# Unpacking the channel weights in the second batch's first two slots and placing its channel groups between theta's products

## The chip, the cores and the metric

The kernel runs on one core of one Trainium2 chip. The metric is the device time of one execution in microseconds (us). A measurement of this kernel repeats to about 0.2%. Engines: PE is TensorE (matrix products), DVE is VectorE, ACT is ScalarE, POOL is GpSimd, SP is SyncE, whose queue starts nearly all transfers here.

## The reference, cut to what matters

For 8 batches of 8 heads, 576 positions and 64 values each: attention with a window of 128 positions and a slope per head; its output x (576 x 512 per batch) goes through a mixing block.

```python
theta = x @ w_theta                              # per batch 576 x 512 @ 512 x 512
zr, zi = x * np.cos(theta), x * np.sin(theta)
y = w_tok_r @ zr + w_tok_i @ zi                  # mixing over the 576 positions
u = x + y
out = u + np.maximum(u @ w_ch, 0.0)              # channels: 512 x 512
```

`w_theta`, `w_tok_r`, `w_tok_i` and `w_ch` arrive as 8-byte floats, which the chip's engines here turn into 4-byte words by integer operations ("unpacking"). Most products are made of three products of shorter words: a matrix is split into a high and a low part, and high x high, high x low and low x high are added.

## The kernel before, in words

Batches follow each other as a pipeline. While batch b+1 does its attention (`attend`), batch b's mixing products (`mix`) stand between that attention's products. Then `turn` of batch b+1 makes x's transposes, theta and the angles, and gives z as a high and a low part. Then batch b's channel products (`channels`) follow.

- `attend` (L814 on) has four slots, one for each pair of heads. A slot runs some steps of mixing, the scores of the next pair (`scores`, then `weigh`: DVE adds the bias and finds the least value, ACT takes the exponential), steps of mixing, `values` of the present pair, `finish` (L583 on: three DVE operations that leave x_sb), and steps of mixing. `flip` (L532 on) turns the next pair's weights: ACT makes the high half (L555), DVE the low half (L558), SP sends both through a transposing transfer to `pt`. `split_low` (L438, L440) makes the low parts of q and k for the pair after the next.
- One step of mixing is three products of 128 x 288 (L77); nine steps are one group, 72 steps a batch. After a group DVE folds the result in (L762), ACT makes u's high part (L764), POOL a scaled copy (L766) and u's low part (L767). How many steps stand where is written out by hand: `FIRST` (L33) for batch 0's mixing, four numbers for each slot. For batch 0 it places 66 steps; the other six stand in the turn of batch 1.
- `turn`'s `run` calls `between` six times: before the first transposes (`columns`), behind the transposes of the next tile of rows for four of the five tiles, and at the end. For batches after the first one, a channel group (12 products of 128 x 288: four with the weights' high part, four with the low part, four with u's low part) is placed at each call, and two more in the attention's last slots. For batch 0 the calls do other work (below), and its eight channel groups run in a row behind the turn of batch 1.
- The channel weights come in four parts of 512 KB (`LATE`). A step of `unpack` takes one part: `apart` (ACT L187, POOL L188), `together` (DVE L194, L197, L202, then ACT L203 sums the rows), and the load of the next part (SP L177). Part 0 is loaded ahead; parts 0 and 1 are unpacked in slot 0, part 2 in slot 1, part 3 in slot 2.
- From the row sums one number follows, the scale s of the channel weights: `sums_first` (DVE L347, L348), `spread_from` (a PE transpose of the peaks, DVE L313, L315), `sums_last` (a PE product with ones, DVE L158, L160, L354, L165). `split_channels` (L358 on) then splits the weights with it: ACT L362 writes wch_hi, DVE L363 wch_lo, each in two halves of 128 x 1024. All this stands in the turn of batch 1, at its calls 2 to 5.

PE runs strictly in the order of the program (`keep_in_program_order`). For the other engines a planner sets the order when the program is built: among what it thinks is ready, the earlier in the program goes first; `issue_after` and `behind_all` let an operation be issued only behind others; `high_priority` brings one forward. Each engine then works through its list in that order. PSUM has two pools: `ps_s` (2 buffers: scores, values, transposes of x) and `ps_m` (4 buffers: mixing, theta, channels, spreads).

Of the kernel before, what the change touches and what calls it, by code (L numbers as in the profile page):

```python
# [17 lines left out]
AF = mybir.ActivationFunctionType  # L18
# [11 lines left out]

DEPTH = 1

FIRST = ((3, 11, 6, 3), (4, 4, 5, 4), (4, 4, 5, 4), (4, 3, 2, 0))  # L33
STEPS, FINISH = ((7, 7, 4, 3), (3, 5, 7, 4), (3, 4, 6, 3)), 250

GROUP = 4
# [17 lines left out]
def attn_moe_kernel(ctx: ExitStack, tc: tile.TileContext, qk_in, vx, wth, wtok, wch_in, band, out):  # L54
    nc = tc.nc
# [35 lines left out]
    def behind_all(some):  # L91
        stack = ExitStack()
        for ins in some:
            stack.enter_context(tc.issue_after(ins.ins))
        return stack
# [249 lines left out]
    def sums_first():  # L345

        nc.vector.tensor_reduce(out=peaks[2][:, :1], in_=csums, axis=mybir.AxisListType.X, op=ALU.max)  # L347
        nc.vector.tensor_scalar(out=peaks[2][:, :1], in0=peaks[2][:, :1], scalar1=2.0 ** (WEXP - 1),  # L348
                                scalar2=2.0 ** -100, op0=ALU.mult, op1=ALU.max)

    def sums_last(diag):

        s = spread_to(diag, 1, "c")
        nc.vector.tensor_scalar(out=ratio[:, 1:2], in0=ratio[:, :1], scalar1=s, scalar2=None, op0=ALU.mult)  # L354
        inverse(ratio[:, 2:3], ratio[:, 1:2])
        return s

    def split_channels(s):  # L358

        for k in range(0, 4, 2):  # L360
            part = slice(k, k + 2)
            nc.scalar.activation(wch_hi[:, part], wch[:, part], AF.Copy, scale=s)  # L362
            nc.vector.scalar_tensor_tensor(out=wch_lo[:, part], in0=wch[:, part], scalar=s, in1=wch_hi[:, part],  # L363
                                           op0=ALU.mult, op1=ALU.subtract)

    def coming(b):
        return [g for g in (2 * b + 3, 2 * b + 4) if g < B * H // GROUP]
# [442 lines left out]
    def step(stream, k=1):  # L810
        for _ in range(k):
            next(stream, None)

    def attend(b, x_sb, mixing, chans, first, behind, lowered):  # L814

        for g in range(H // 2):
            p = b * H // 2 + g
            pair = first.pop(0)
            new = None
            if p + DEPTH < pairs:  # L820
                new = Pair(p + DEPTH)
                first.append(new)
            def scores(tiles):
                if new is not None:
                    with tc.issue_after(lowered.ins) if b == 1 and g == 0 else nullcontext():
                        new.scores(tiles, behind)

            steps = STEPS[min(g, 2)] if b > 1 else FIRST[g]
            step(mixing, steps[0])
            if g == 1:  # L830
                spread_scales(b - 1, diag)
            ahead = p + DEPTH + 1
            made = split_high(ahead, raw.pop(ahead)) if ahead < pairs else None
            for tiles in SCORES:
                scores(tiles)
            if made is not None:
                with tc.issue_after(new.weighed.ins):
                    parts[ahead] = split_low(made)
                    prepare(ahead + 1)
            if new is not None and not new.early:  # L840
                new.flip(0)
                if g:
                    new.flip(1)
            step(mixing, steps[1])
            if g == 0:
                diag = spread_first(b - 1)
            step(mixing, steps[2])
            pair.values()
            with tc.high_priority(FINISH):
                done = pair.finish(x_sb)  # L850
            if new is not None and (new.early or g == 0):
                new.flip(0 if new.early else 1, done)
            step(mixing, steps[3])
            if new is not None and new.early:
                new.flip(1)
            with tc.issue_after(done.ins):
                if new is not None:
                    new.heads[0].ready()
                if b == 1 and g == 0:
                    with behind_all(new.exps):  # L860
                        step(late)
            if g >= 2 and b > 1:
                step(chans)
            if new is not None:
                with tc.issue_after(done.ins):
                    done = new.heads[1].ready() or done
                    for low in lows:
                        after(low(), done)
                    if b == 1 and g < 3:
                        with behind_all(new.exps + [new.copied]):  # L870
                            step(late)
            else:
                for low in lows:
                    low()
            lows.clear()
            if new is not None and not new.early:
                sent[:] = [new.sent]
            if g == (1 if b == 1 else 0) or g == 2:
                g_v = 2 * b + 3 + g // 2
                if g_v < B * H // GROUP:  # L880
                    with behind_all(sent):
                        load_values(g_v)
# [88 lines left out]
    for b in range(B):  # L971
        chans = channels(b, st[b])
        mixing = mix(st[b])
        if b + 1 < B:
            x_sb = xp.tile([128, NT, DM], F32, name="x_sb")
            attend(b + 1, x_sb, mixing, chans, first, st[b]["turned"], st[b]["lowered"])
            if b:
                for _ in mixing:
                    pass
            if first:  # L980
                latest = first[-1].exps
            st[b + 1]["exps"] = latest
            calls, diags = [], []

            def between():
                calls.append(None)
                n = len(calls)
                if b:
                    step(chans)
                elif n == 1:  # L990
                    step(mixing, 3)
                elif n == 2:
                    for _ in mixing:
                        pass
                    for low in lows:
                        low()
                    lows.clear()
                    sums_first()
                elif n == 3:
                    diags.append(spread_from(peaks[2], 1, "c"))  # L1000
                elif n == 4:
                    diags.append(sums_last(diags[0]))
                elif n == 5:
                    split_channels(diags[1])

            turn(x_sb, st[b + 1])(between)
            for _ in chans:
                pass
        else:
            step(mixing, 45)  # L1010
            for _ in range(3):
                step(chans)
                step(mixing, 9)
            for _ in mixing:
                pass
            for _ in chans:
                pass
# [52 lines left out]
```

## Time and profile before

| what | value |
|---|---|
| time before, median of 3 runs | 631.06 us (630.17 to 631.55) |
| the profiled execution's own time | 630.1 us |
| its span, from first to last instruction | 628.3 us |
| PE busy | 600.3 us (96%) |
| DVE busy | 527.6 us (84%) |
| ACT busy | 486.3 us (77%) |
| POOL busy | 198.7 us (32%) |
| attention of batch 1 (four slots) | about 91 to 142 us in the span |
| turn of batch 1 | about 140 to 162 us |
| channels of batch 0 | 162.2 to 173.9 us |

Times in the rows are counted from the first instruction. A row of a timeline gives the start, the duration, the engine, the line, the operation and its tiles; what stands in brackets at its end is the idle time of the engine before it, and what ended it. Matmuls overlap, so what a matmul costs is the distance between starts. "Granted clock" is the share of full speed that TensorE was given.

### The profile page before, as it was taken

How to read it: one execution, taken by the hardware profiler on the slowest of the kernel's cores; microseconds unless marked ns; L12 is line 12 of the kernel's file. 1: busy time of each engine (PE TensorE's matmuls, PEld its weight loads, DVE VectorE, ACT ScalarE, POOL GpSimd, SP SyncE). 2: the span in 40 equal slices, each digit the busy share in tenths (PEclk: the TensorE clock that was granted, in tenths of full speed). 3: DMA queues.
4: the chain of work that ended last, by engine and by line, in shares of the span. 5: the costliest groups of instructions: out<-in, count | busy, mean ns of one | idle time of the engine just before them, and what ended most of it. 6: DMA issues, size and time to landing. Idle time of an engine off the chain costs nothing.

```text
span 628.3 us, 14876 instructions
## 1 busy us (share of the span) xinstructions
PE 600.3 (96%) x5727; PEld 493.3 (79%) x5727; DVE 527.6 (84%) x1350; ACT 486.3 (77%) x917; POOL 198.7 (32%) x252
## 2 busy tenths in 40 slices
PE   5799799988899999999999999999999999999997
PEld 3688578867688878888788878888788878887776
DVE  4788888999999988998899889997899879956733
ACT  3889878788688779896989689886998799727710
POOL 4433303442314402432224411541225322530200
PEclk9789989999999999999999999999999999999999
DMA  8952102794148930897059910995069802751001
GB/s 317 355 188 85 53 25 75 164 230 81 39 116 196 225 73 20 199 193 171 21 100 220 215 50 26 228 207 118 30 148 183 179 29 75 113 87 39 20 20 57
DMA packets 137847, 78.10 MB, mean 124 GB/s; under 512 B 110768, under 2 KB 127280, under 8 KB 137776
## 3 DMA queue, kind: packets, MB, share of 16 engines
q1 hardware_dynamic: 137776, 77.15, 51.0%
q8 instruction: 45, 0.74, 0.5%
q14 instruction: 26, 0.21, 0.1%
HBM read 40.44 MB, written 9.44 MB: 79 GB/s over the span
## 4 chain that ended last, share of the span: by engine, by line
PE 55%; DVE 18%; ACT 14%; DMA 3%; issue 2%; DVEq 0%; ACTq 0%
PE mm L77 44%; PE ps L77 9%; DMA pt<-hl 3%; DVE hl L558 2%; PE ps L102 2%; ACT back L530 2%; ACT hl L555 2%; ACT front L530 1%; ACT g L675 1%; DVE front L527 1%; DVE f L671 1%; ACT g L674 1%; DVE g L685 1%; DVE f L685 1%; DVE z_lo L624 1%
## 5 line engine op out<-in xcount | busy, mean ns | idle before, releaser
L77 PE MATMUL mm<-wtk_hi,z_hi 128*128 128x288 f16 x576 | 165.1, 287 | 0.0
L77 PE MATMUL mm<-wtk_lo,z_hi 128*128 128x288 f16 x576 | 164.7, 286 | 0.0
L77 PE MATMUL mm<-wtk_hi,z_lo 128*128 128x288 f16 x576 | 164.7, 286 | 0.0
L77 PEld LDWEIGHTS <-z_hi 128*128 128x128 f16 x1152 | 108.7, 98 | 29.4 <-issue 0.6
L766 POOL TENSOR_SCALAR us<-xtf,fixed 128x288 f32<-128x288 f32 x56 | 80.4, 1438 | 107.5 <-DVE xtf L762 105.1
L77 PE MATMUL mm<-u,wch_hi 128*128 128x288 f16 x512 | 81.1, 287 | 0.0
L530 ACT ACTIVATE front<-front,fixed 128x256 f32<-128x256 f32 (+2 forms) x160 | 60.5, 444 | 20.4 <-DVE fixed L527 20.1
L77 PEld LDWEIGHTS <-z_lo 128*128 128x128 f16 x576 | 56.4, 98 | 14.2
L77 PEld LDWEIGHTS <-wch_hi 128*128 128x128 f16 x512 | 48.1, 98 | 18.0 <-issue 6.9
L764 ACT ACTIVATE u<-xtf,fixed 128x288 f16<-128x288 f32 x64 | 33.5, 525 | 32.7 <-DVE xtf L762 32.7
L530 ACT ACTIVATE back<-back,fixed 128x256 f32<-128x256 f32 x128 | 56.4, 495 | 2.1 <-DVE fixed L527 2.1
L767 POOL TENSOR_TENSOR u<-us,u 128x288 f16<-128x288 f32 x56 | 43.0, 782 | 44.9 <-DVE vl L461 21.5
L77 PE MATMUL mm<-wth_hi,x_hi 128*128 128x512 f32 x160 | 47.5, 419 | 3.9 <-ACT x_hi L646 2.5
L624 POOL TENSOR_TENSOR z_lo<-g,z_hi 128x512 f16<-128x512 f32 x14 | 16.5, 1179 | 109.3 <-ACT z_hi L622 109.3
L77 PE MATMUL ps<-vh,pt 128*128 128x65 f16 x936 | 47.8, 194 | 2.8 <-DMA pt<-hl 1.6
L77 PEld LDWEIGHTS <-pt 128*128 128x128 f16 x1404 | 46.4, 98 | 4.9 <-DMA pt<-hl 2.3
L77 PE MATMUL ps<-kh,qh 64*128 64x256 f32 (+1 forms) x304 | 47.3, 351 | 1.8 <-DVE x_sb L596 0.9
L77 PE MATMUL ps<-vl,pt 128*128 128x64 f16 x468 | 45.9, 193 | 0.0
L762 DVE SCALAR_TENSOR_TENSOR xtf<-mm,fixed,xtf 128x288 f32<-128x288 f32 x64 | 32.0, 510 | 15.1 <-PE mm L77 15.1
L77 PE MATMUL mm<-wth_lo,x_hi 128*128 128x512 f32 x160 | 44.5, 399 | 0.0
L795 DVE SCALAR_TENSOR_TENSOR xtf<-mm,fixed,xtf 128x288 f32<-128x288 f32 x64 | 32.7, 512 | 13.1 <-PE mm L77 12.6
L77 PE MATMUL mm<-u,wch_lo 128*128 128x288 f16 x256 | 41.8, 286 | 0.0
(186 smaller groups left out, 1442.2 us busy)
## 6 DMA issues: line engine op xcount, KB each, us to landing
vb<-in_vx_dram SPq DMA_DIRECT2D x16, 650.0 KB, 5.2
out_dram<-xtf SPq DMA_DIRECT2D x64, 144.0 KB, 1.8
qr<-in_qk_dram SPq DMA_DIRECT2D x26, 320.0 KB, 3.0
kr<-in_qk_dram SPq DMA_DIRECT2D x26, 288.0 KB, 3.8
xtf<-in_wch_dram SPq DMA_DIRECT2D x4, 512.0 KB, 3.8
qh<-in_qk_dram SPq DMA_DIRECT2D x6, 320.0 KB, 5.8
kh<-in_qk_dram SPq DMA_DIRECT2D x6, 288.0 KB, 6.1
xtf<-in_wtok_dram SPq DMA_DIRECT2D x3, 576.0 KB, 9.2
```

The source lines that it names most:

```text
L77: ins = nc.tensor.matmul(*args, **kw)
L102: ins = nc.tensor.transpose(*args)
L530: self.exps.append(nc.scalar.activation(sb, sb, AF.Exp, bias=least, scale=-1.0))
L555: self.copied = nc.scalar.activation(hl[:, 0], src, AF.Copy, scale=2.0 ** PEXP)
L558: self.lowered = nc.vector.scalar_tensor_tensor(out=hl[:, 1], in0=src, scalar=2.0 ** PEXP, in1=hl[:, 0], op0=ALU.mult, op1=ALU.subtract)
L624: low = engine.tensor_tensor(out=z_lo[:, c, :], in0=z, in1=z_hi[:, c, :], op=ALU.subtract)
L685: nc.vector.scalar_tensor_tensor(out=z, in0=x_sb[:, i, :], scalar=zs[:, c:c + 1], in1=z, op0=ALU.mult, op1=ALU.mult)
L762: nc.vector.scalar_tensor_tensor(out=xtf[:, m, cs], in0=y_ps[:, :HALF], scalar=st["back"], in1=xtf[:, m, cs], op0=ALU.mult, op1=ALU.add)
L764: nc.scalar.activation(u_hi[:, m, cs], xtf[:, m, cs], AF.Copy, scale=up)
L766: nc.gpsimd.tensor_scalar(out=us[:, m, cs], in0=xtf[:, m, cs], scalar1=up, scalar2=None, op0=ALU.mult)
L767: lows.append(lambda m=m, cs=cs: nc.gpsimd.tensor_tensor(out=u_lo[:, m, cs], in0=us[:, m, cs], in1=u_hi[:, m, cs], op=ALU.subtract))
L795: nc.vector.scalar_tensor_tensor(out=xtf[:, e, cs], in0=o_ps[:, :HALF], scalar=down, in1=xtf[:, e, cs], op0=ALU.mult, op1=ALU.max)
```

## The change

Part 2 is unpacked in slot 1 at the first head and part 3 in slot 1 at the second (before: slot 1, second head, and slot 2, second head). `sums_first` follows in slot 1. `spread_from` stands behind slot 2's `finish`, `sums_last` behind the first mixing steps of slot 3, and the two halves of `split_channels` stand at slot 3's first and second head. All 72 mixing steps of batch 0 are now in the attention: slot 3 has (4, 4, 4, 3) in place of (4, 3, 2, 0). The calls of `between` in batch 1's turn place 0, 1, 1, 2, 2 and 1 channel groups of batch 0, and the eighth follows the turn.

```diff
-FIRST = ((3, 11, 6, 3), (4, 4, 5, 4), (4, 4, 5, 4), (4, 3, 2, 0))
+FIRST = ((3, 11, 6, 3), (4, 4, 5, 4), (4, 4, 5, 4), (4, 4, 4, 3))
...
-    def split_channels(s):
-
-        for k in range(0, 4, 2):
-            part = slice(k, k + 2)
-            nc.scalar.activation(wch_hi[:, part], wch[:, part], AF.Copy, scale=s)
-            nc.vector.scalar_tensor_tensor(out=wch_lo[:, part], in0=wch[:, part], scalar=s, in1=wch_hi[:, part],
-                                           op0=ALU.mult, op1=ALU.subtract)
+    def split_channels(s, k):
+
+        part = slice(k, k + 2)
+        nc.scalar.activation(wch_hi[:, part], wch[:, part], AF.Copy, scale=s)
+        nc.vector.scalar_tensor_tensor(out=wch_lo[:, part], in0=wch[:, part], scalar=s, in1=wch_hi[:, part],
+                                       op0=ALU.mult, op1=ALU.subtract)
...
             step(mixing, steps[0])
+            if b == 1 and g == 3:
+                one = sums_last(diag)
...
                 done = pair.finish(x_sb)
+            if b == 1 and g == 2:
+                with tc.issue_after(done.ins):
+                    diag = spread_from(peaks[2], 1, "c")
...
-                if b == 1 and g == 0:
+                if b == 1 and g < 2:
                     with behind_all(new.exps):
                         step(late)
+                elif b == 1 and g == 3:
+                    with behind_all(new.exps):
+                        split_channels(one, 0)
...
-                    if b == 1 and g < 3:
+                    if b == 1 and g < 2:
                         with behind_all(new.exps + [new.copied]):
                             step(late)
+                            if g:
+                                sums_first()
+                    elif b == 1 and g == 3:
+                        with behind_all(new.exps + [new.copied]):
+                            split_channels(one, 2)
...
             attend(b + 1, x_sb, mixing, chans, first, st[b]["turned"], st[b]["lowered"])
-            if b:
-                for _ in mixing:
-                    pass
+            for _ in mixing:
+                pass
...
-            calls, diags = [], []
-
-            def between():
-                calls.append(None)
-                n = len(calls)
-                if b:
-                    step(chans)
-                elif n == 1:
-                    step(mixing, 3)
-                elif n == 2:
-                    for _ in mixing:
-                        pass
-                    for low in lows:
-                        low()
-                    lows.clear()
-                    sums_first()
-                elif n == 3:
-                    diags.append(spread_from(peaks[2], 1, "c"))
-                elif n == 4:
-                    diags.append(sums_last(diags[0]))
-                elif n == 5:
-                    split_channels(diags[1])
-
-            turn(x_sb, st[b + 1])(between)
+            counts = [] if b else [0, 1, 1, 2, 2, 1]
+            turn(x_sb, st[b + 1])(lambda: step(chans, counts.pop(0) if counts else 1))
             for _ in chans:
                 pass
```

## Rows read from the trace of the kernel before

**Rows 1.** Windows: stretch; length, busy of PE, PEld, DVE, ACT, POOL; PEclk, DMA, GB/s

```profile
130.00:142.00 12.00, 8.91 (x120) 7.12 (x117) 11.90 (x37) 10.33 (x24) 5.49 (x9) 1.00 1.07 222
142.00:162.00 20.00, 16.75 (x85) 13.29 (x85) 18.50 (x31) 16.97 (x28) 5.04 (x8) 1.00 0.32 53
162.00:174.00 12.00, 12.00 (x99) 9.47 (x98) 10.81 (x17) 7.90 (x14) 4.08 (x4) 1.00 0.19 64
...
220.00:240.00 20.00, 20.00 (x120) 16.00 (x119) 16.86 (x27) 15.95 (x28) 3.54 (x4) 1.00 0.30 64
```

**Rows 2.** Timeline of PE, 136 to 160 us: the rows ahead of which it waited

```profile
136.82 0.19 PE L77 MATMUL ps<-vh,pt 128*128 128x65 f16 x1 [1.05 <-DVE fixed L527]
...
138.21 0.20 PE L77 MATMUL ps<-vh,pt 128*128 128x65 f16 x1 [0.87 <-DMA pt<-hl]
...
142.38 0.33 PE L102 MATMUL ps<-fixed,x_sb 128*128 128x128 f32 x1 [1.29 <-DVE x_sb L596]
...
145.20 1.20 PE L77 MATMUL mm<-wth_hi,x_hi 128*128 128x512 f32 x4 [0.95 <-DVE x_hi L641]
...
159.25 1.20 PE L77 MATMUL mm<-wth_hi,x_hi 128*128 128x512 f32 x4 [1.92 <-ACT x_hi L646]
```

**Rows 3.** Timeline of ACT in the turn of batch 1

```profile
152.87 2.18 ACT L362 ACTIVATE wch_hi<-wch,fixed 128x1024 f16<-128x1024 f32 x2
```

**Rows 4.** Timeline of DVE, 137 to 157 us: end of slot 3, and the split

```profile
137.98 0.81 DVE L438 SCALAR_TENSOR_TENSOR ql<-qr,qh 128x640 fp32r<-128x640 f32 x1
...
141.07 0.15 DVE L591 SCALAR_TENSOR_TENSOR fixed<-ps,fixed 128x10 f32<-128x10 f32 x1
...
142.25 1.00 DVE L461 SCALAR_TENSOR_TENSOR vl<-vb,fixed,vh 128x320 f16<-128x320 f32 x2
143.17 1.22 DVE L558 SCALAR_TENSOR_TENSOR hl<-back,hl 128x1024 f16<-128x1024 f32 x1
144.31 0.51 DVE L762 SCALAR_TENSOR_TENSOR xtf<-mm,fixed,xtf 128x288 f32<-128x288 f32 x1
...
154.03 2.48 DVE L363 SCALAR_TENSOR_TENSOR wch_lo<-wch,fixed,wch_hi 128x1024 f16<-128x1024 f32 x2 [0.43 <-ACT wch_hi L362]
```

**Rows 5.** Timeline of DVE, 147 to 154 us: operations of the channel scale

```profile
147.48 0.29 DVE L313 TENSOR_REDUCE fixed<-mm 128x1 f32<-128x128 f32 x1 [0.35 <-PE mm L102]
...
153.21 0.21 DVE L354 TENSOR_SCALAR fixed<-fixed 128x1 f32<-128x1 f32 x1
153.45 0.15 DVE L165 TENSOR_SCALAR fixed<-fixed 128x1 int32<-128x1 int32 x1
```

**Rows 6.** Timeline of DVE, 129 to 136 us: its last idle time, and part 3's unpacking

```profile
129.99 1.23 DVE L558 SCALAR_TENSOR_TENSOR hl<-back,hl 128x1024 f16<-128x1024 f32 x1 [0.41 <-ACT hl L555]
...
133.54 0.68 DVE L194 SCALAR_TENSOR_TENSOR xtf<-xtf 128x512 int32<-128x512 int32 x1
...
134.41 0.95 DVE L197 SCALAR_TENSOR_TENSOR wch<-xtf 128x512 int32<-128x512 int32 x1
```

**Rows 7.** Timeline of PE, 142 to 174 us: starts that price products

```profile
142.55 0.29 PE L77 MATMUL mm<-wtk_hi,z_hi 128*128 128x288 f16 x1
...
143.65 0.60 PE L102 MATMUL ps<-fixed,x_sb 128*128 128x128 f32 x4
...
147.17 0.27 PE L102 MATMUL mm<-fixed,peak 128*128 128x128 f32 x1
147.28 0.60 PE L102 MATMUL ps<-fixed,x_sb 128*128 128x128 f32 x4
147.64 1.18 PE L77 MATMUL mm<-wth_hi,x_hi 128*128 128x512 f32 x4
...
173.94 0.29 PE L77 MATMUL mm<-wtk_hi,z_hi 128*128 128x288 f16 x1
```

**Rows 8.** Windows in the turn of batch 0, columns as in rows 1

```profile
74.00:76.00 2.00, 0.77 (x5) 0.54 (x5) 2.00 (x4) 2.00 (x4) 0.00 (x0) 0.92 0.00 0
76.00:82.00 6.00, 4.73 (x16) 3.85 (x17) 5.05 (x17) 4.63 (x8) 1.29 (x3) 0.50 0.27 87
```

## The prediction

> **What bounds the kernel now.** I read the page first: PE is busy for nearly the whole span, DVE is next. Shares over a span hide stages, so I cut the stretch that the change touches into windows. From 162 us on PE is busy without a gap, in the channel groups that run in a row as well as in batch 2's turn, where channel groups already stand between theta's products and DVE still has 3 us in 20 to spare. Ahead of 162 us it is not: PE lacks 3.1 us in the end of the attention and 3.3 us in the turn, and in the first of these windows DVE is busy for 11.90 of 12 us [rows 1]. So the change can only win in those 6 us, and DVE is the engine to watch there.
>
> The timeline of PE then gives each wait: 1.05 us ahead of slot 3's values (for DVE's weighing), 0.87 us within them (for the transposed weights), 1.29 us for x_sb, 0.95 us for theta's first operand, 1.92 us for theta's last operand; together 6.08 us [rows 2]. The last one is made by the split itself: ACT is held for 2.18 us by wch_hi and comes to the operand only behind that [rows 3]. If every wait went and none came, the time would fall by 6.1 us; that is the ceiling.
>
> **The change part by part.**
>
> *Mixing steps.* Nine products of mixing take 143.65 - 142.55 = 1.10 us, so a product costs 0.122 us and a step 0.37 us [rows 7]. Three of the six moved steps go ahead of slot 3's values (1.1 us, into the waits of 1.05 and 0.87 us), three stay where they were in PE's order, between the values and the first transposes. PE's own work is the same; only waits can differ.
>
> *Channel groups.* They are the same 96 products with the same evictions and stores. SP's stores come earlier, into a stretch where the transfer engines are used for 0.32 of the time [rows 1]. They now cover the wait of 1.92 us, and ACT no longer has the split in front of theta's operands. But the first group stands behind the first transposes, so PE, which keeps the program's order, can't pass it: if wch_lo isn't there, everything in the turn waits. Behind that wait stand all of theta's products, and with them ACT's angles and DVE's z.
>
> *Part 3 of the weights.* Its two long DVE operations, 0.68 and 0.95 us [rows 6], are done a slot earlier. DVE was full in both places, so this only moves other DVE work back, then lets it catch up: nothing by slot 3's end. POOL's operation of it goes with it; POOL is half idle [rows 1]. The load on SP stands one head earlier in the same slot, between the same two transposing transfers: nothing.
>
> *The scale.* L313 and two operations like L354, three like L165 and starts between them: 0.29 + 2 x 0.21 + 3 x 0.15 = 1.16 us, about 1.1 on DVE, formerly in the turn [rows 5], now ahead of slot 3's finish. DVE's one gap in that stretch, 0.41 us [rows 6], can take some of it, so I take 0.7 us of delay; the ends are 0 and 1.1.
>
> *The split.* L363 twice, 2.48 us on DVE [rows 4], goes from the middle of the turn to between the end of slot 3 and the first channel group.
>
> **The sum: when can the first group begin?** Before, slot 3's finish ends at 142.25, where the vl pair starts (0.92 us to the next start) [rows 4]. With the scale's 0.7 that is 142.95. Then vl 0.92, the two halves of wch_lo 2.48, the last mixing group's eviction 0.42 (it can fall behind; ends 0 and 0.42). The low half hl of the next pair's weights, 1.14 us [rows 4], isn't needed before batch 2 but is ready about then. The rows point both ways: vl, later in the program, went ahead of it before, yet the second half of the split is tied behind the same ACT copy that releases hl. I take half, 0.57; ends 0 and 1.14. Together 147.34. PE needs the second half of wch_lo only from its seventh product, 6 x 0.122 = 0.73 us in, so the group can begin at **146.6 us**. Ends: 142.25 + 0.92 + 2.48 - 0.73 = 144.9, and 143.35 + 0.92 + 2.48 + 0.42 + 1.14 = 148.3.
>
> When must it begin for no change? Before, from the second tile's transposes to the end of the channels it is 173.94 - 143.65 = 30.29 us. In that, theta began at 145.20, though four transposes take 0.36 us (147.28 to 147.64), so 1.19 us were lost; then 1.92 us; and the two small products of the scale, 0.11 us each (147.17 to 147.28) [rows 2, 7], now lie in the attention. What is left, 26.96 us, is PE's work from the first group to the end of the channels. Taken from 173.94, break-even is **147.0 us**. Before, PE has no wait behind this point [rows 1], so the difference goes through to the end.
>
> So the forecast is 146.6 - 147.0 = -0.4 us: waits of 3.1 us in the turn go, and a single one of about that size appears ahead of the first group. Against the profiled execution's own 630.1 us (span 628.3 and 1.8 around it) that is 629.7; the median of the runs shown, 631.06, is 1.0 higher, and on that scale the time is **630.7 us**. The bounds give 629.0 (-2.1) to 632.4 (+1.3).
>
> **A long wait and the clock.** In batch 0's turn PE was busy for 0.77 of 2 us, and the granted clock, 0.92 in that window, was 0.50 for the next 6 us [rows 8]; that is 1.2 in place of 2.4 GHz. The forecast leaves PE idle from about 143.1 (x_sb at 142.95 and the transposes) to 146.6, 3.5 us. At half the clock for 6 us, up to 3 us would be lost: -0.4 + 3.0 = +2.6 us. Against it: PE is nearly full ahead of that wait, and the five waits of before, 1.05 to 1.92 us long, left 1.00 in their windows [rows 1, 2].
>
> The Trainium skill, "TensorE: Matmul & The Clock Gate", section "Part 1: The HAM clock gate (the "warmup" mystery)", says that the array has these two rates and drops to the lower one after it has stood idle. By that rule the sum would be the +2.6, not the -0.4. The trace agrees that the clock halves behind a thin stretch, by the 0.50 above; whether one wait behind full work does it, no row here shows.
>
> **The rivals.**
>
> 1. *The split gets ahead* (faster). DVE's low parts ql and kl for batch 2's first slot (0.81 us, and I take its twin at 0.6 as an estimate from it) lie ahead of slot 3's finish [rows 4], and so does part of hl, and none is due before batch 2. If the planner, with more on the list, lets all of them slip behind the split, the group begins 0.57 + 1.4 earlier, at 144.6: -2.4 us, **628.7 us**. For it: vl did overtake hl. Against: ql and kl are earlier in the program, and stood early before.
>
> 2. *The product with ones holds slot 3* (slower). It stands in PE's order ahead of slot 3's scores, and its operand comes from L313 and L315, behind slot 2's finish. From slot 2's values to that product PE has eight steps, 2.9 us. If DVE in that time must do two halves of hl (2.28), the finish (142.25 - 141.07 = 1.18), part 3 (1.6), vl (0.92) and the two small ones (0.5) [rows 4 to 6], that is 6.5 us, and PE waits 3.6 us with the scores behind it. Slot 3 had 1.92 us of waits [rows 2], of which the three steps take 1.1; with the 0.7 by which DVE is later anyway PE can lose 1.5 us free of charge. That is the point from which it decides; beyond it 2.1 us come through: -0.4 + 2.1 = +1.7, **632.8 us**. For it: DVE is full in that stretch. Against: `finish` is brought forward, and the planner may put the small ones right behind it.
>
> 3. *The clock falls* (slower): +2.6, **633.7 us**, as above.
>
> 4. *One wait for another, no more.* If wch_lo comes just when all the old waits would have been spent, the change only renames them: **631.1 us**.
>
> **How the numbers follow.** A measurement of this kernel can tell about 0.2%, 1.26 us, from no change: 629.8 to 632.3 is the same. The forecast has 0.50; of its own range, 629.0 to 632.4, I give 0.15 to faster, 0.32 to the same, 0.03 to slower. Rival 1 has 0.20 (faster), rival 2 0.15 and rival 3 0.07 (slower), rival 4 0.08 (same). So faster 0.35, same 0.40, slower 0.25. For 8 times in 10 the range must reach rival 1 with some scatter, 628.0, and rival 2 with some, 633.2; most of rival 3 is left out.
>
> **What would show it.** Right: no wait ahead of theta's last product; one wait ahead of the first channel product, released by DVE's L363, from about 143 to 146.6; channels ending near 173.5; PE full from there. L313 and L315 near 133 us with no long wait of PE ahead of slot 3's scores. Wrong by rival 1: that wait under 2 us, ql and kl behind L363. By rival 2: a PE wait over 1.5 us at the product with ones, released by L315, and slot 3's finish after 144. By rival 3: PEclk under 1.00 in 143 to 155. My sum fails if DVE isn't full up to the split, or if PE, once started, waits again in the turn for x_lo or a free PSUM buffer.

## The result, and the profile after

The changed kernel takes **637.57 us** (median of 4 runs, 636.54 to 639.62) where the kernel before took 630.86 on the same chip: a ratio of 1.0118, 95% interval 1.0092 to 1.0144. It is slower by 6.7 us, beyond the range of the prediction and beyond every rival. The profiled execution took 636.5 us.

The page's busy times, the whole span:

```profile
span 634.8 us, 14875 instructions
PE 602.7 (95%) x5727; PEld 493.4 (78%) x5727; DVE 526.4 (83%) x1350; ACT 486.5 (77%) x917; POOL 194.7 (31%) x252
```

The span is 6.5 us longer than before (628.3); PE is busy for 2.4 us more with as many products (600.3 before). So 4.1 us are idle time of PE and 2.4 us are the same products taking longer. Both are net figures of two single executions: slot 1's values, which stand ahead of everything that was moved, begin 1.6 us earlier in this one (112.58 us) than in that of before (114.18); in all twelve traces they begin between 112.58 and 115.51 us. Windows of the changed kernel show where (stretch; length, busy of PE, PEld, DVE, ACT, POOL; PEclk, DMA, GB/s):

```profile
126.00:132.00 6.00, 0.61 (x20) 0.48 (x16) 5.93 (x11) 5.96 (x12) 1.48 (x3) 0.84 0.71 205
132.00:138.00 6.00, 4.86 (x25) 3.25 (x26) 2.08 (x7) 0.54 (x1) 2.47 (x3) 0.59 1.05 226
138.00:144.00 6.00, 6.00 (x80) 5.18 (x79) 5.26 (x25) 4.43 (x11) 0.56 (x2) 1.00 0.06 20
144.00:150.00 6.00, 3.89 (x54) 2.53 (x50) 5.93 (x10) 5.96 (x11) 2.18 (x4) 1.00 0.93 194
150.00:156.00 6.00, 4.28 (x15) 3.44 (x16) 3.66 (x6) 1.92 (x4) 3.29 (x3) 0.55 0.54 112
156.00:162.00 6.00, 6.00 (x32) 4.42 (x31) 4.53 (x6) 3.63 (x7) 0.00 (x0) 0.88 0.07 25
162.00:186.00 24.00, 24.00 (x176) 19.17 (x175) 19.72 (x44) 20.19 (x35) 4.72 (x4) 1.00 0.11 38
```

From 126 to 132 us PE stands nearly still while DVE and ACT are full. Then the roles swap: from 132 to 138 PE works at a granted clock of 0.59 and DVE has little to do, where before it had 11.90 of 12 us in 130 to 142 [rows 1]. A second hole with a low clock lies in 144 to 156. From 162 us on PE is full, as predicted. The timeline of PE names the holes:

```profile
133.15 0.47 PE L102 MATMUL mm<-fixed,peak 128*128 128x128 f32 x1 [6.54 <-DVE peak L348]
133.41 0.44 PE L77 MATMUL mm<-wtk_hi,z_hi 128*128 128x288 f16 x1
...
138.07 0.28 PE L77 MATMUL mm<-fixed 128*128 128x1 f32 x2
...
147.24 0.42 PE L77 MATMUL mm<-u,wch_hi 128*128 128x288 f16 x2 [0.18 <-ACT wch_hi L361]
148.14 0.42 PE L77 MATMUL mm<-u,wch_lo 128*128 128x288 f16 x2 [0.48 <-DVE wch_lo L362]
151.72 0.66 PE L77 MATMUL mm<-u,wch_lo 128*128 128x288 f16 x2 [3.17 <-DVE wch_lo L362]
```

(Behind L360 this kernel's line numbers are one lower than before: L362 here is L363 there.) The five waits of before [rows 2] are gone. In their place stands one of 6.54 us, at the transposition of the peaks, a product of 0.11 us; and 0.18 + 0.48 + 3.17 = 3.83 us inside the first channel group. The 24 mixing products behind the first wait take 138.07 - 133.41 = 4.66 us, 0.194 each, where 0.122 is usual [rows 7].

Why were the peaks (L348) so late? The timelines of ACT and then of DVE:

```profile
129.60 0.72 ACT L430 ACTIVATE qh<-qr 128x640 fp32r<-128x640 f32 x1
130.23 0.55 ACT L458 ACTIVATE vh<-vb,fixed 128x320 f16<-128x320 f32 x1
130.68 0.65 ACT L431 CAST kh<-kr 128x576 fp32r<-128x576 f32 x1
131.24 0.62 ACT L203 ACTIVATE xtf<-wch 128x512 f32<-128x512 f32 x1
```
```profile
129.44 0.28 DVE L202 TENSOR_TENSOR wch<-wch,fixed 128x128 f32<-128x128 f32 x1
...
131.83 1.00 DVE L460 SCALAR_TENSOR_TENSOR vl<-vb,fixed,vh 128x320 f16<-128x320 f32 x2
132.75 0.15 DVE L347 TENSOR_REDUCE peak<-fixed 128x1 f32<-128x4 f32 x1
132.94 0.15 DVE L348 TENSOR_SCALAR peak<-peak 128x1 f32<-128x1 f32 x1
133.66 0.29 DVE L313 TENSOR_REDUCE fixed<-mm 128x1 f32<-128x128 f32 x1 [0.57 <-PE mm L102]
...
138.39 0.16 DVE L158 TENSOR_SCALAR fixed<-mm 128x1 int32<-128x1 int32 x1 [3.49 <-PE mm L77]
```

Part 3's unpacking ends with DVE's L202, then ACT's row sums (L203), then DVE's L347 and L348. On ACT the sums stand behind the next pair's qh, vh and kh, on DVE the peaks behind vl, all of it work that nobody waits for yet. These account for 1.5 us (L202's end at 129.72 to L203's start) and 0.8 us (from the end of the sums to L347). Of the rest, 3.1 us pass before L202 is done: PE stands still from 126.61 us on. PE, idle since slot 2's values, can't pass the transposition: the eight mixing steps stand behind it. Then DVE in its turn has nothing to do for 3.49 us, because slot 3's scores are late.

### The profile page after: what moved, and what is told of

It reads as the page before. It is cut to its first block, busy times and chain, and to the rows that moved or that the text cites. A ratio compares the mean times of both kernels' runs of the same rounds, so it can differ in the third digit from the quotient of the medians.

```text
span 634.8 us, 14875 instructions
## 1 busy us (share of the span) xinstructions
PE 602.7 (95%) x5727; PEld 493.4 (78%) x5727; DVE 526.4 (83%) x1350; ACT 486.5 (77%) x917; POOL 194.7 (31%) x252
## 4 chain that ended last, share of the span: by engine, by line
PE 58%; DVE 18%; ACT 13%; issue 2%; DMA 2%; DVEq 0%; ACTq 0%
PE mm L77 46%; PE ps L77 10%; DVE hl L557 2%; PE ps L102 2%; DMA pt<-hl 2%; ACT back L529 2%; ACT hl L554 1%; ACT front L529 1%; DVE front L526 1%; DVE f L670 1%; DVE g L684 1%; ACT g L674 1%; ACT g L673 1%; DVE f L684 1%; DVE z_lo L623 1%
## 5 line engine op out<-in xcount | busy, mean ns | idle before, releaser
L765 POOL TENSOR_SCALAR us<-xtf,fixed 128x288 f32<-128x288 f32 x56 | 78.6, 1406 | 111.8 <-DVE xtf L761 110.6
L77 PE MATMUL mm<-u,wch_hi 128*128 128x288 f16 x512 | 82.5, 288 | 0.2 <-ACT wch_hi L361 0.2
L766 POOL TENSOR_TENSOR u<-us,u 128x288 f16<-128x288 f32 x56 | 41.4, 754 | 54.5 <-DVE vl L460 24.2
```

Source lines behind the costliest of these rows:

```text
L77: ins = nc.tensor.matmul(*args, **kw)
L765: nc.gpsimd.tensor_scalar(out=us[:, m, cs], in0=xtf[:, m, cs], scalar1=up, scalar2=None, op0=ALU.mult)
L766: lows.append(lambda m=m, cs=cs: nc.gpsimd.tensor_tensor(out=u_lo[:, m, cs], in0=us[:, m, cs], in1=u_hi[:, m, cs], op=ALU.subtract))
```

## The experiments

Two parts of the change came under suspicion: the place of the peaks' transposition in PE's order (first hole), and the place of the split, on ACT and DVE, ahead of theta's first operands (second hole). Beside them the clock, the order of the channel groups and part 3's move were to be told apart. The table gives every run: its ratio to before, measured on the same chip (and not exactly the quotient of the two medians), and from its trace two stretches of the path on which PE's order is followed, A from slot 2's values to the first transposes of batch 1's turn, B from there to the start of batch 1's mixing. (The stretch ahead, from slot 1's to slot 2's values, is 12.22 to 12.24 us in all of them.)

| kernel | median us (runs) | ratio [95%] | A | B |
|---|---|---|---|---|
| before | 630.2 to 630.9 | 1 | 14.19 | 33.34 |
| changed | 637.57 (4) | 1.0118 [1.0092, 1.0144] | 21.20 | 34.30 |
| e1, peaks later | 633.54 (6) | 1.0049 [1.0024, 1.0073] | 16.04 | 34.46 |
| e10, split in the turn | 634.04 (4) | 1.0055 [1.0034, 1.0075] | 20.74 | 31.35 |
| e7, both | 629.58 (12) | 0.9983 [0.9961, 1.0005] | 16.25 | 30.11 |
| e3, groups last | 639.44 (4) | 1.0142 [1.0116, 1.0167] | 21.18 | 35.40 |
| e5, e1 with later groups | 633.94 (5) | 1.0062 [1.0039, 1.0085] | 16.04 | 34.81 |
| e2, first wait filled | 636.24 (4) | 1.0089 [1.0059, 1.0119] | 20.21 | 34.36 |
| e6, e1 with its wait filled | 631.81 (10) | 1.0031 [1.0008, 1.0055] | 16.04 | 32.85 |
| e4, unpacking alone | 630.67 (12) | 1.0002 [0.9983, 1.0021] | 14.28 | 32.93 |
| e8, scale and split in the turn | 631.82 (11) | 1.0020 [1.0007, 1.0034] | 14.04 | 34.84 |
| e9, split alone, from before | 629.32 (12) | 0.9978 [0.9963, 0.9993] | 13.40 | 33.72 |

In the changed kernel three mixing steps (1.10 us) and the scale's two products (0.22) lie in A instead of B, so "nothing gained or lost" would read 15.51 and 32.02 there (the rows from the changed kernel to e6; in e8 only the steps have moved, 15.29 and 32.24). By that the changed kernel loses 5.7 us in A and 2.3 in B; the start that is 1.6 us earlier in its trace hides part of these 8.0 us in the span.

### e1: the peaks' transposition later

```diff
             step(mixing, steps[0])
-            if b == 1 and g == 3:
-                one = sums_last(diag)
...
+            if b == 1 and g == 3:
+                diag = spread_from(peaks[2], 1, "c")
             step(mixing, steps[2])
             pair.values()
+            if b == 1 and g == 3:
+                one = sums_last(diag)
             with tc.high_priority(FINISH):
                 done = pair.finish(x_sb)
-            if b == 1 and g == 2:
-                with tc.issue_after(done.ins):
-                    diag = spread_from(peaks[2], 1, "c")
```

> The changed kernel with two of PE's instructions moved: the transposition of the peaks goes from behind slot 2's values to behind slot 3's scores and their four mixing steps, the product with ones from ahead of slot 3's scores to behind slot 3's values. Theory A (place): PE reached the transposition 6.5 us before its operand, so the place alone made the wait, and the fall of the clock behind it (24 mixing products in 4.7 us where 2.9 is usual). Then the wait of 6.54 us is gone, the clock stays at 1.00 up to slot 3's end, and slot 3's finish comes some 7 us earlier; part returns as a longer wait of the first channel group for the split, so 632 to 634 us. Theory B (VectorE's work up to the split bounds the stretch wherever PE waits): the wait turns up elsewhere in full, 636 to 638 us.

633.54 us, as theory A said: 4 of the 6.7 us come back, and A falls from 21.20 to 16.04. PE's timeline:

```profile
135.20 0.28 PE L102 MATMUL mm<-fixed,peak 128*128 128x128 f32 x1
...
145.53 0.66 PE L77 MATMUL mm<-u,wch_hi 128*128 128x288 f16 x2 [2.54 <-ACT wch_hi L361]
...
148.06 0.66 PE L77 MATMUL mm<-u,wch_lo 128*128 128x288 f16 x2 [0.35 <-DVE wch_lo L362]
```

The transposition waits for nothing now. Only the place of the scale's two products, and of the small DVE operations that go with them, was altered; the chain that makes their operand is the same. So the first hole is their place in PE's order. The second stays: the first channel group still waits for the split, with the clock at 0.56 from 144 to 150 us, and B is no shorter (34.46).

### e2: the first wait filled with unread products

```diff
             if b == 1 and g == 2:
+                unread(done, 50)
                 with tc.issue_after(done.ins):
```

The edit adds 50 products that nobody reads, right ahead of the transposition.

> The changed kernel with 50 products of the identity (128 x 256, two-byte, 0.12 us each, 6 us in all, their result unused) ahead of the transposition of the peaks, in the 6.54 us in which PE stood idle; nothing else is moved. It tells the price of the clock from that of the wait. Theory A with the clock as a part of its own: the wait stays, but the 24 mixing products behind it take 2.9 us in place of 4.7, and the scores of slot 3 start 1.7 us earlier: 635.5 to 636.2 us. Theory B: the first channel group waits for the split until the same moment, 637 to 638 us.

```profile
132.00:138.00 6.00, 4.69 (x42) 3.82 (x40) 4.26 (x11) 2.94 (x6) 1.12 (x2) 1.00 0.96 166
```
```profile
136.18 0.33 PE L102 MATMUL mm<-fixed,peak 128*128 128x128 f32 x1 [1.31 <-DVE peak L348]
136.34 0.29 PE L77 MATMUL mm<-wtk_hi,z_hi 128*128 128x288 f16 x1
...
139.28 0.28 PE L77 MATMUL mm<-fixed 128*128 128x1 f32 x2
```

With the array kept busy the clock stays at 1.00 (the first fence, a window) through the wait and behind it, and the 24 mixing products take 139.28 - 136.34 = 2.94 us in place of 4.66. The operand comes no earlier (the second fence, PE's timeline), so the delay itself stays. In this execution it even comes 0.8 us later, counted from slot 2's values (127.01 to 136.18, where the changed kernel has 124.80 to 133.15): ACT waits 1.08 us for a transfer of kr, and the row sums stand behind that. A falls by 1.0 us, the median by 1.3, to the upper end of theory A; the two intervals don't quite separate this from the changed kernel. The clock is the smaller part of the first hole: 1.72 us in those 24 products, beside a wait of 6.54.

### e3 and e5: the order of the channel groups

```diff
-            counts = [] if b else [0, 1, 1, 2, 2, 1]
+            counts = [] if b else [0, 0, 0, 0, 0, 0]
```

> The changed kernel with all eight channel groups behind the turn of batch 1, as before the change; all else as changed. The three waits of the first group (0.18, 0.48 and 3.17 us) stand ahead of theta's products in the changed kernel, and theta's first eight products ran at half the clock (3.6 us where 2.0 is usual). If these are a cost of their own, they go, and PE enters theta some 6 us earlier; some comes back because nothing then covers theta's operands: 632 to 634 us. If the order of the groups is not a cost (ACT and VectorE need that time for the angles anyway): 636.5 to 638 us.

e3 is no faster, 639.44 us, above both of the forecasts; its interval overlaps with the changed kernel's. PE's timeline shows that the wait only moved:

```profile
154.35 2.08 PE L77 MATMUL mm<-wth_hi,x_hi 128*128 128x512 f32 x4 [4.81 <-DVE x_hi L640]
```

The groups were not at fault. ACT and DVE do the split ahead of theta's first operand (L640, x_hi) whether a channel group asks for it or not; without a group there, PE waits 4.81 us for x_hi. e5 is e1 with its counts at 0, 0, 1, 2, 2, 2, so with no group ahead of theta's first products, and one group less up to the fifth call:

> The first experiment, and the channel groups one call later: 0, 0, 1, 2, 2, 2 at the six calls and one behind the turn. If the two waits are separate costs, both go: 628 to 631 us, at or below the kernel before. If the split bounds both, the first group only waits in a later place: 632 to 635 us.

633.94 us, as e1 (633.54), and the same wait in a later place, 4.95 us ahead of theta. Where the groups stand is worth nothing that can be told as long as the split stands ahead of x_hi.

### e7 and e10: the split in the turn, behind theta's operands

```diff
-                elif b == 1 and g == 3:
-                    with behind_all(new.exps):
-                        split_channels(one, 0)
...
-                    elif b == 1 and g == 3:
-                        with behind_all(new.exps + [new.copied]):
-                            split_channels(one, 2)
...
-            counts = [] if b else [0, 1, 1, 2, 2, 1]
+            counts = [] if b else [0, 0, 0, 0, 2, 3]
+            calls = []
+
+            def between():
+                calls.append(None)
+                if not b and len(calls) in (3, 4):
+                    with behind_all([st[1]["high"], st[1]["rest"]]):
+                        split_channels(ones_s[0], 2 * (len(calls) - 3))
+                step(chans, counts.pop(0) if counts else 1)
```

`high` and `rest` are the copies of x that theta's next products read. `ones_s` holds the scale. e7 has this and the edit of e1; e10 has this alone, with the peaks where the change put them.

> The first experiment with the split taken out of slot 3 and placed in the turn, each half behind the operands of theta's next tile on ScalarE and VectorE (tiles 1 and 2), and the channel groups at 0, 0, 0, 0, 2, 3 with three behind the turn. Theory: what is left of the loss in the first experiment comes from the split standing ahead of theta's first operands on ScalarE and VectorE, so that PE stands idle 3 us with a fall of the clock whatever the place of the groups. Then no wait over 1 us is left in the turn, the waits of 0.95 and 1.92 us of the kernel before are gone as well, and the time is 628 to 630 us, below the kernel before. If the moves inside the attention (part 3, the scale) cost the rest: 632 to 634 us.

> The changed kernel, but only the second cause is undone: the split's halves go to the turn, behind x's operand copies, the channel groups behind them; the transposition of the peaks stays directly behind slot 2's values. Theory (two causes that add): of the changed kernel's +6.7 us the split's share of about 4.0 (629.58 in place of 633.54) goes and the peaks' share stays, so about 633.2 us, with a PE wait near 6 us at the peaks' transposition, DVE idle for over 2 us behind it, and no wait over 2 us ahead of theta. Rival A (the late scores make the split late; the split costs nothing of its own): about 637 us. Rival B (the peaks' wait only costs because the split stands behind it; slack in the turn takes it): about 630 us.

The four kernels make a square. Moving the transposition is worth 1.18 - 0.49 = 0.69% with the split in slot 3, and 0.55 + 0.17 = 0.72% with it in the turn. Moving the split is worth 1.18 - 0.55 = 0.63% and 0.49 + 0.17 = 0.66%. So the two causes add, 4.4 and 4.1 us of 630, as far as intervals of 0.2 to 0.26% to either side can tell (the medians alone, each less before of its chip, give 3.8 and 4.0, and 3.4 and 3.5). They sit in different stretches: the first changes A (by 5.2 and 4.5 us), the second B (by 3.0 and 4.4). "Moving the split" takes the channel groups along; e3 and e5 say that their place by itself gave nothing. The theory of e10, about 633.2, is met (634.04); both of its rivals are some 3 us or more off. PE's timeline of e10, then its DVE:

```profile
134.32 0.48 PE L102 MATMUL mm<-fixed,peak 128*128 128x128 f32 x1 [6.38 <-DVE peak L348]
...
148.94 0.77 PE L102 MATMUL ps<-fixed,x_sb 128*128 128x128 f32 x5 [1.74 <-DVE x_sb L595]
150.20 1.59 PE L77 MATMUL mm<-wth_hi,x_hi 128*128 128x512 f32 x4 [0.49 <-DVE x_hi L640]
```
```profile
139.10 0.16 DVE L158 TENSOR_SCALAR fixed<-mm 128x1 int32<-128x1 int32 x1 [3.02 <-PE mm L77]
```

The long wait and DVE's hole behind it stay; nothing over 1.74 us is left in the turn, though the clock is 0.72 from 150 to 156 us. In e7 neither is there, and its interval against before holds 1: with both causes undone the rest of the change is worth nothing that can be told. e7's time is the 628 to 630 us of its theory, but "below the kernel before" isn't shown, and two waits over 1 us are left in its turn (1.04 and 1.25). It also pays for the clock in slot 3. PE's timeline, then a window:

```profile
135.42 0.39 PE L77 MATMUL ps<-kh,qh 64*128 64x256 f32 x2 [1.56 <-DVE x_sb L595]
```
```profile
132.00:138.00 6.00, 4.44 (x41) 3.32 (x39) 5.97 (x24) 4.91 (x13) 2.43 (x3) 0.86 0.85 163
```

Behind this wait of 1.56 us twelve mixing products take 139.18 - 136.33 = 2.85 us, 0.24 each, twice the usual 0.122: 1.4 us.

### e6: e1 with the second wait filled

```diff
+                if not b and len(calls) == 2:
+                    unread(st[1]["flipped"], 30)
```

> The first experiment (transposition of the peaks later) with 30 unused products of the identity (0.12 us each, 3.6 us) between the first transposes of the turn and the first channel group, where PE waited for the split; no operation of VectorE or ScalarE is moved ahead of the split. In the first experiment the granted clock was 0.56 behind that wait and theta's first products ran at half the rate. If the clock is a cost of its own there, the time falls by 1 to 2 us against the first experiment's 633.5, to about 632; if not, it stays.

631.81 us against e1's 633.54 (the intervals overlap), B down by 1.6. Thirty products fill the time in which PE waited for the split. In PE's timeline theta's first eight products then take 153.09 - 151.14 = 1.95 us, as before (1.97) [rows 7]; in the changed kernel, at a clock of 0.55, they take 157.41 - 153.85 = 3.56. The operand isn't earlier (the group's wait for wch_lo ends 6.9 us behind the first transposes in both): the gain is the clock's. PE's timelines, the changed kernel and then e6:

```profile
153.85 2.05 PE L77 MATMUL mm<-wth_hi,x_hi 128*128 128x512 f32 x4
...
157.41 0.66 PE L77 MATMUL mm<-u,wch_hi 128*128 128x288 f16 x4
```
```profile
151.14 1.18 PE L77 MATMUL mm<-wth_hi,x_hi 128*128 128x512 f32 x4
...
153.09 0.66 PE L77 MATMUL mm<-u,wch_hi 128*128 128x288 f16 x4
```

### e4: the unpacking alone

```diff
-                if b == 1 and g == 0:
+                if b == 1 and g < 2:
...
-                    if b == 1 and g < 3:
+                    if b == 1 and g < 2:
```

This is the kernel before with part 2 and part 3 both in slot 1.

> The kernel before with one part of the change alone: parts 2 and 3 of the channel weights are unpacked in slot 1's two heads; the scale, the split, the mixing steps and the channel groups stay in the turn as before. If the move of part 3 is free, as the prediction said (VectorE is full in both places), the time is within 1 us of the kernel before. If it delays slot 2's finish and with it the scores of slot 3 (a wait for x_sb of 1.7 us stands there in the first experiment, 0.26 before) and that comes through, 1 to 2 us slower.

630.67 against 630.2 us, ratio 1.0002 [0.9983, 1.0021]: free. The wait for x_sb ahead of slot 3's scores rises from 0.26 to 1.40 us. Of the later ones, the 1.05 us ahead of slot 3's values are gone and the 1.29 us ahead of the turn are 0.80; the other three stay (0.91, 1.05, 1.93):

```profile
134.73 0.38 PE L77 MATMUL ps<-kh,qh 64*128 64x256 f32 x2 [1.40 <-DVE x_sb L596]
```

### e8 and e9: from the kernel before, the split moved with (e8) and without (e9) the mixing steps

e9 leaves the mixing steps, moves the scale's two steps one call forward and the split's halves to calls 3 and 4, and places two and three groups at calls 5 and 6:

```diff
-                elif n == 3:
                     diags.append(spread_from(peaks[2], 1, "c"))
-                elif n == 4:
+                elif n == 3:
                     diags.append(sums_last(diags[0]))
-                elif n == 5:
-                    split_channels(diags[1])
+                    with behind_all([st[1]["high"], st[1]["rest"]]):
+                        split_channels(diags[1], 0)
+                elif n == 4:
+                    with behind_all([st[1]["high"], st[1]["rest"]]):
+                        split_channels(diags[1], 2)
+                else:
+                    step(chans, n - 3)
```

e8 puts all 72 steps into the attention as well, and the scale's steps one call earlier still:

```diff
-FIRST = ((3, 11, 6, 3), (4, 4, 5, 4), (4, 4, 5, 4), (4, 3, 2, 0))
+FIRST = ((3, 11, 6, 3), (4, 4, 5, 4), (4, 4, 5, 4), (4, 4, 4, 3))
...
+                if not b and n == 1:
                     diags.append(spread_from(peaks[2], 1, "c"))
-                elif n == 4:
+                elif not b and n == 2:
                     diags.append(sums_last(diags[0]))
```

> The kernel before, with the unpacking where it was, all 72 mixing steps in the attention, the whole scale at the turn's first calls, the split's halves at calls 3 and 4 behind x's operand copies, and two and three channel groups at calls 5 and 6. Theory (the split belongs behind theta's operands, the rest of the change is worth little): the waits of 1.92 us at theta's last operand and of about 1 us for vh's weights go; one of about 1 us comes in the turn, where the six steps no longer stand ahead of the scale: 628.5 us, -2 us. Rival (those six steps covered the turn's first waits, x's copy and the scale's chain, and the groups come too late to replace them): 630 to 632 us.

> The kernel before with the split alone moved: the scale's two steps one call earlier, the split's halves at calls 3 and 4 behind x's operand copies, two channel groups at call 5 and three at call 6. Theory: the 1.92 us wait at theta's last operand goes and nothing comes in its place, so about 628.5 us (-1.9). Rival (the two products of the scale, a call earlier, wait for DVE with theta's first operands behind them, about 1 us each): 630.0 us or more, waits of 1 us or more at the transposition of the peaks or the product with ones.

e8's theory fell, its rival holds: 631.82 us, 0.2% slower than before. PE's timeline, then DVE's:

```profile
147.00 0.58 PE L77 MATMUL mm<-fixed 128*128 128x1 f32 x2 [3.23 <-DVE fixed L315]
```
```profile
144.65 1.65 DVE L557 SCALAR_TENSOR_TENSOR hl<-back,hl 128x1024 f16<-128x1024 f32 x1
146.21 0.28 DVE L313 TENSOR_REDUCE fixed<-mm 128x1 f32<-128x128 f32 x1
146.41 0.41 DVE L640 TENSOR_TENSOR x_hi<-ps,x_hi 128x256 fp32r<-128x256 f32 x1
146.75 0.20 DVE L315 TENSOR_SCALAR fixed<-fixed 128x1 f32<-128x1 f32 x1
```

It is the first hole again, in small: the product with ones waits 3.23 us because its operand (L315) stands in DVE's list behind vl, a mixing eviction, hl (not needed before the next attention) and x_hi, and theta's products queue behind it. e9 keeps six mixing steps for the turn and asks for this product a call later; there the wait is 0.70 us.

e9 has the lowest time, 629.32 us, ratio 0.9978 [0.9963, 0.9993], and is the only one whose interval lies below 1 (e7's overlaps with it); it beats both kernels, by 1.4 us against before. The wait of 1.92 us ahead of theta's last operand is gone. The forecast of -1.9 is a little high: PE's timeline has a longer wait for x_sb (1.29 before) and a new one for the scale, and behind the first the clock is low for a while (the second fence, a window):

```profile
141.84 0.43 PE L102 MATMUL ps<-fixed,x_sb 128*128 128x128 f32 x1 [2.08 <-DVE x_sb L595]
...
148.40 0.38 PE L77 MATMUL mm<-fixed 128*128 128x1 f32 x2 [0.70 <-DVE fixed L315]
```
```profile
142.00:148.00 6.00, 5.62 (x23) 3.75 (x22) 4.74 (x8) 3.66 (x9) 3.29 (x3) 0.72 1.01 174
```

In its profiled execution A and B together are only 0.4 us shorter than before (13.40 + 33.72 against 14.19 + 33.34); where the other 1.0 us of the medians' difference lies is left open.

## Why the prediction was wrong

**The step that failed is "The scale".** It counted the scale's DVE work (0.7 us of delay) and priced its two products at 0.11 us each, and never asked what those products wait for. Rival 2 did ask, but for the wrong one: "From slot 2's values to that product PE has eight steps". That holds for the product with ones. The transposition of the peaks comes first in PE's order, directly behind slot 2's values, with no step between. In the trace of before slot 2's values end at 128.3 us, while the prediction's own sign of being right had L313, which follows the transposition, near 133. So the whole of part 3's chain (L202, L203, L347, L348) had to be done by then, and wasn't by 6.54 us. The diff showed the place. The Trainium skill, "TensorE: Matmul & The Clock Gate", section "Step-by-step: what each phase is for", says that only weight loads are pulled ahead and matmuls stay in program order. The trace agrees: 24 mixing products stand behind the 6.54 us and then run without a wait.

**The sum, with what it measured.** Slot 2's values begin 1.61 us earlier in this execution (124.80 for 126.41), which is added here to compare. Slot 3's finish ended at 146.34 + 1.61 = 147.95, not at 142.95: 5.0 us late, nearly all from the first hole: A is 5.7 us over 15.51 here, and 0.5 us in e1. From there to the end of wch_lo the sum had 4.39 us; DVE's timeline has 151.66 - 146.34 = 5.32:

```profile
146.34 0.54 DVE L460 SCALAR_TENSOR_TENSOR vl<-vb,fixed,vh 128x320 f16<-128x320 f32 x1
146.80 1.28 DVE L362 SCALAR_TENSOR_TENSOR wch_lo<-wch,fixed,wch_hi 128x1024 f16<-128x1024 f32 x1
148.00 1.22 DVE L557 SCALAR_TENSOR_TENSOR hl<-back,hl 128x1024 f16<-128x1024 f32 x1
149.13 0.55 DVE L460 SCALAR_TENSOR_TENSOR vl<-vb,fixed,vh 128x320 f16<-128x320 f32 x1
149.59 0.51 DVE L761 SCALAR_TENSOR_TENSOR xtf<-mm,fixed,xtf 128x288 f32<-128x288 f32 x1
150.02 1.64 DVE L362 SCALAR_TENSOR_TENSOR wch_lo<-wch,fixed,wch_hi 128x1024 f16<-128x1024 f32 x1
151.59 0.41 DVE L640 TENSOR_TENSOR x_hi<-ps,x_hi 128x256 fp32r<-128x256 f32 x1
```

All of hl came in between (1.13, the upper end; half was taken), the mixing eviction too, and the second half of wch_lo took 1.64. So the group could run through from 151.72 - 0.73 + 1.61 = 152.6, against a break-even of 147.0: +5.6 us. Its last six products and the transposes took 2.13 us (151.72 to 153.85) for 1.09 at full clock, and theta's first eight 3.56 for 1.97: +1.0 and +1.6. Together +8.2; the trace has +7.97 from slot 2's values to batch 1's mixing (A and B together). The break-even was sound; what was put into it was not. The sum also has a slip, which decides nothing here: the late end of the group's start, 148.3, leaves out the 0.73 us that the other end takes off. It would be 147.6, and the upper bound 631.7 in place of 632.4.

**"DVE is full up to the split"**, named as a condition of the sum, failed: 3.49 us idle ahead of L158. The delay by 0.7 us assumed that DVE sets the pace through slot 3; PE did, from the moment it stood still.

**"ACT no longer has the split in front of theta's operands"** was wrong: both engines still do it ahead of x_hi (the last two rows above); moving it with the groups gave 3.4 to 4.1 us by the square. Behind the group's wait for wch_lo stands one for x_hi, which e3 lays bare (4.81 us); the sum saw one of the two.

**Rival 3, the clock**, had 0.07 as a case of its own. It came with the long waits, twice. The prediction had left open whether one wait behind full work does it: here one of 6.54 us was followed by 0.59. Its price of up to 3 us is of the right size: 1.7 us at the first hole, 2.6 at the second. The Trainium skill, "TensorE: Matmul & The Clock Gate", section "Part 1: The HAM clock gate (the "warmup" mystery)", calls the lower rate the default, which activity lifts. The trace agrees in that the clock is back at 1.00 in 138 to 144 us, behind the 24 products.

**Right:** the five waits that the change was to win (all vanish, though others take their place), part 3's move (e4: free), PE full behind the turn, and the wait for wch_lo ahead of the first channel group as the new limit of the turn. **The chances:** the rivals were weighed as if one excluded the other. Here each long wait brought the clock down with it, and the split ahead of x_hi adds to both; the range had held them one at a time.

## What to carry to other kernels

When a small product moves in an engine's order that is kept, list the whole chain of its operand, with each link's place in its engine's list, and ask what stands between it and the last work that is sure to run: its own duration says nothing. A step moved ahead of a stage can hold that stage by two engines at once; look for the operands that queue behind it, not only for its reader. And add a lower clock to every forecast that leaves TensorE idle for several microseconds: in these runs the long waits and the clock were one case.

## What the runs showed of the hardware

One wait of 6.54 us behind full work brought the granted clock down to 0.59 in the window behind it; 3.17 us behind two short ones, to 0.55. The length of a wait alone doesn't tell: 1.74 us in e1 and the five of before, up to 1.92 [rows 1, 2], left 1.00, while 2.08 us in e9 gave 0.72, and 1.56 us in e7 0.86, with twelve products at half the usual rate behind it. Filling the waits with unread products kept the clock at 1.00 (e2 at the first hole, e6 all through the turn) and gave back 1.3 and 1.7 us with the operand no earlier. Those intervals overlap with the unfilled kernels', so the clock's price rests on the products' rates (4.66 for 2.94 us, 3.56 for 1.95) more than on the medians. Whether part 3's row sums could go earlier in ACT's list was not tried; by the rows of the first hole it could take some 1.5 of the 6.54 us (an estimate).
